# Weight conversion in slices of 768 columns on two engines, and TensorE in program order from the start

## The chip, the cores and the metric

The kernel runs on one core of a Trainium2 chip. The metric is the device time of one execution in microseconds (us). A core has a matrix engine (PE in the profile, with its weight loads as PEld), a vector engine (DVE), a scalar engine (ACT), a general engine (GpSimd, POOL in the profile) and a sync engine (SP) whose queue issues the transfers. Each engine works through its own instructions in order; semaphores make one wait for another.

## The reference

Three stages follow each other: a linear-attention recurrence per batch and head, a gated product, and a second feed-forward stage. All inputs are drawn with `np.random.randn` or `rand`; the weights of the two last stages arrive as float64.

```python
# B=4, H=8, S=768, D=48
for t in range(S):                       # r, k, v, w: [B,H,S,D] float32, u: [H,D]
    y[:, :, t] = r_t @ (state + (u * k_t) v_t)
    state = w_t[:, None] * state + k_t v_t
x = y.transpose(0, 2, 1, 3).reshape(B * S, H * D)      # 3072 x 384
h = ((x @ w1) * (x @ w2)) @ w3                         # w1, w2: 384 x 1024, w3: 1024 x 1024
x = h @ w_out                                          # 1024 x 384
h = x @ w_in                                           # 384 x 2048
g = h * np.clip(h + 3, 0, 6) / 6
return g @ w_out2                                      # 2048 x 384
```

## The kernel before

**Weights.** A float64 weight arrives as two 32-bit words. The kernel converts it on the chip to a float32 bit pattern: `conv`, from the high word `hi` and the low word `lo` of a raw slice. It knows two ways. The *mixed* one uses ACT twice (L98 the magnitude, L99 the sign), DVE three times (L100, L101, L102) and POOL once (L104, a product with the sign). The other one uses ACT once (L106) and DVE four times (L108, L109, L111, L113). The first slice of w3 and of w_out and every second slice of the others go the second way. Weights that are used in several-pass products are then split into a high part by ACT (L116) and a low part by DVE or POOL (L117); a product of split operands is three matmuls (`mm3`, L120 to L122). A `Stream` holds a list of slices and takes each through load, first half (the ACT part) and second half; at most `ahead` slices are between load and end. Slices are 384 or 512 columns.

**Stage A** computes w34 = w3 @ w_out with plain float32 matmuls (L386) while w_out and w3 are converted, and runs the first attention blocks beside it. The w3 slices are `raw_w`/`w3f` in the profile, the w_out ones `raw_wo`/`wo`. Attention is 32 blocks m (a pair of heads, half of a sequence): `load` (wkr, rkv), `prep` (scans e and f, products, the mask A on POOL), `do_kn` (L187), `do_sc` (L198), `do_kv` (L210), `do_y` (L234). Four blocks make one x tile `xt` of 384 tokens.

**Stage B** is the first of eight token blocks bi of the gated product: for each of eight column groups f the products `ab` into two banks, a copy by ACT (L482), the product by DVE (L487), the split into gh and gl (L116, L117), then `out1` with w34 into three accumulators, which ACT copies out at the end (L424). While bi = 0 runs, w1 and w2 (`w12`) are converted. **Stage C** is bi 1 to 5 with attention beside them. **Stage D** is the end of bi 6 and bi 7, with w_in (`wi`) and w_out2 (`wo2`) converted beside them. **Stage E** is the second feed-forward stage, with no conversion left except a little at its start.

**What sets the order.** In stages B to E the PE instructions stand in program order; in stage A a scheduler places them by a simulated time. The other engines are always placed by the scheduler. SP issues the transfers in its order, and a load waits there until its buffer is free.

Of the kernel before, what the change touches and what calls it, by code (L numbers as in the profile page):

```python
# [32 lines left out]
LEAST = float(np.array(0x38000000, np.uint32).view(np.float32))  # L33
MOST = float(np.array(0x47EFFFFF, np.uint32).view(np.float32))
# [8 lines left out]
def pool_split(bi, f):  # L43

    return bi in (0, 1, 7) and f % 2 and f < 7


def build(nc, tc, a):
# [30 lines left out]
    stg = pool("stg", bufs=6, side="left")  # L79
# [12 lines left out]
    def conv(f, raw, late, mixed):  # L92

        lo, hi = raw[..., 0], raw[..., 1]
        fi, ff = f, f.bitcast(F32)
        hf = hi.bitcast(F32)
        if mixed and not late:
            ACT.activation(ff, hf, AF.Abs, scale=2.0 ** -112)  # L98
            ACT.activation(hf, hf, AF.Sign)  # L99
            V.tensor_scalar(out=ff, in0=ff, scalar1=MOST_S, scalar2=None, op0=ALU.min)  # L100
            V.tensor_scalar(out=lo, in0=lo, scalar1=29, scalar2=None, op0=ALU.logical_shift_right)  # L101
            V.scalar_tensor_tensor(out=fi, in0=fi, scalar=3, in1=lo, op0=ALU.logical_shift_left, op1=ALU.bitwise_or)  # L102
        elif mixed:
# [44 lines left out]
    def prep(m):  # L148
# [8 lines left out]
        P_.tensor_copy(stat[:, 1, m], zcols(d1v[i], ZC))  # L157
# [134 lines left out]
    raws, fs = {}, {}  # L292

    def w_load(key, src, n):

        t = stg.tile([128, n, 2], I32, name=f"raw_{key}", tag="raw")
        if len(src.shape) == 3:
            k = src.shape[0]
            nc.sync.dma_start(t.rearrange("p (k m) t -> p k (m t)", k=k), src.rearrange("k p m -> p k m").bitcast(I32))
        else:  # L300
            nc.sync.dma_start(t, src.bitcast(I32).rearrange("p (m t) -> p m t", t=2))
        raws[key] = t

    def w_conv(key, n, late, mixed, hi=None, lo=None, eng=None, dst=None):
        if not late:
            fs[key] = stg.tile([128, n], I32, name=f"f_{key}", tag="f") if dst is None else dst()
            conv(fs[key], raws[key], False, mixed)
        else:
            conv(fs[key], raws.pop(key), True, mixed)
            if dst is None:  # L310
                split(hi, lo, fs.pop(key).bitcast(F32), eng)
# [34 lines left out]

    ear = pool("ear", bufs=2, side="left")
# [4 lines left out]
    def w3_at(q, c0, c1):  # L352
        if q not in w3s:
            w3s[q] = ear.tile([128, 512], I32, name=f"w3f_{q}", tag="w3f", bufs=6)
        return w3s[q][:, c0:c1]

    for q in range(2 * NF1):
        fh, j = divmod(q, NF1)
        if fh == 0:
            args.append((f"wo_{j}", DM, a["w_out"][j], j > 0, None, None, None, lambda j=j: wo[:, j]))  # L360
        for c0, c1 in (((0, 512),) if q else ((0, 128), (128, 512))):
            args.append((f"w3_{q}_{c0}", c1 - c0, a["w3T"][j, :, 512 * fh + c0:512 * fh + c1], q > 0, None, None, None,
                         lambda q=q, c0=c0, c1=c1: w3_at(q, c0, c1)))
    e3 = Stream(args, 4)
# [16 lines left out]


    def w34(fh, j, f4, w3):
        g = fh * 4 + f4
        ps = bank[g % 5][:, :DM]
        mm(ps, w3[:, 128 * f4:128 * f4 + 128], wo[:, j].bitcast(F32), start=j == 0, stop=j == NF1 - 1)  # L386
        if j == NF1 - 1:
            split(w34h[:, g], w34l[:, g], ps)

    e3.upto(3)  # L390
    first = prep(0)
    for q in range(2 * NF1):
        fh, j = divmod(q, NF1)
# [10 lines left out]
    w12p = pool("w12p", bufs=1, side="left")  # L404
    w12h = w12p.tile([128, NF1, 2, KT, 128], F32R, name="w12h")
    w12l = w12p.tile([128, NF1, 2, KT, 128], F32R, name="w12l")
    w12 = Stream([(f"w12_{f}_{s}", DM, a["w2" if s else "w1"][:, :, 128 * f:128 * f + 128], s,
                   w12h[:, f, s].rearrange("p k m -> p (k m)"), w12l[:, f, s].rearrange("p k m -> p (k m)"),
                   P_ if s == 0 else None)
                  for f in range(NF1) for s in range(2)])  # L410
    w12.upto(2)
# [31 lines left out]
    def win_start():  # L443
# [4 lines left out]
        p2["l"] = wp.tile([128, NF2, KT, 128], F32R, name="wil")  # L448
        p2["wi"] = Stream([(f"wi_{j}", DM, a["w_in"][:, :, 128 * j:128 * j + 128], j % 2,
                            p2["h"][:, j].rearrange("p k m -> p (k m)"), p2["l"][:, j].rearrange("p k m -> p (k m)"),  # L450
                            None if j % 2 else P_) for j in range(NF2)])
        p2["wo"] = Stream([(f"wo2_{j}", DM, a["w_out2"][j], j % 2, wo2h[:, j], wo2l[:, j], None if j % 2 else P_)
                           for j in range(NF2)], 1)

# [277 lines left out]
```

## Time and profile before

| what | us |
|---|---|
| median of 3 runs | 962.64 (961.16 to 965.11) |
| profiled execution | 961.57 |
| its span in the trace | 959.8 |
| PE busy | 880.5 (92%) |
| DVE busy | 556.1 (58%) |
| ACT busy | 374.3 (39%) |
| POOL busy | 257.9 (27%) |

The profiled execution lies 1.07 us below the median; its span is 1.8 us shorter than its time. Busy shares are averages over stages that are limited by different engines, so the rows below are taken stage by stage. On DVE, ACT and POOL an instruction's listed duration overlaps the next one's a little; the distance from one start to the next is what an instruction costs when the engine never waits.

### The profile page before, as it was taken

The page shows a single profiled execution, that of the slowest core. Times are in us where ns is not written, and L with a number is a line of the kernel's source. Part 1 is how long each engine was busy: PE and PEld are TensorE (multiplying, and loading weights), DVE is VectorE, ACT ScalarE, POOL GpSimd, SP SyncE. Part 2 cuts the span into 40 slices and gives each one's busy share as a digit, 9 for nine tenths or more (in the row PEclk, how much of TensorE's full clock was granted, in tenths as well). Part 3 has the DMA queues.
Part 4 walks back from the last instruction along what each step waited for, and adds up shares of the span by engine and source line. Part 5 has one row for each costly group of instructions (what it writes and reads, how often), then busy time and mean ns, then how long its engine had stood idle before and what let it go on. Part 6 is the DMA issues. An engine that isn't in the chain of part 4 may idle for free.

```text
span 959.8 us, 13483 instructions
## 1 busy us (share of the span) xinstructions
PE 880.5 (92%) x5074; PEld 744.9 (78%) x5074; DVE 556.1 (58%) x938; ACT 374.3 (39%) x876; POOL 257.9 (27%) x297
## 2 busy tenths in 40 slices
PE   4678677999999999999987899999999999999997
PEld 2344566899889999998877788888888888888885
DVE  8999799565665757575599833433433433333332
ACT  5445553333323333333456533333433433333332
POOL 4988556343332424242155400000000000000000
PEclk9798899999999999999998999999999999999998
DMA  9685466451434334342146410100100000000001
GB/s 277 212 242 167 140 201 186 107 155 56 138 95 125 112 103 134 107 130 79 38 127 211 137 37 1 33 33 0 66 1 1 34 1 0 33 1 1 34 0 37
DMA packets 40762, 86.18 MB, mean 90 GB/s; under 512 B 4352, under 2 KB 20208, under 8 KB 40688
## 3 DMA queue, kind: packets, MB, share of 16 engines
q1 hardware_dynamic: 40688, 85.23, 29.8%
q8 instruction: 42, 0.69, 0.3%
q14 instruction: 32, 0.26, 0.1%
HBM read 66.34 MB, written 9.44 MB: 79 GB/s over the span
## 4 chain that ended last, share of the span: by engine, by line
PE 69%; DVE 17%; DMA 7%; issue 2%; POOL 2%; ACT 2%; SPq 0%; ACTq 0%; POOLq 0%; DVEq 0%
PE bank L120 21%; PE bank L121 21%; PE bank L122 21%; DMA wkr<-in_wkr 4%; PE abank L234 3%; PE abank L198 2%; DVE f L159 1%; DMA raw_w<-in_w 1%; DVE e L155 1%; POOL w3f L104 1%; DMA raw_wo<-in_w_out 1%; DVE w12l L117 1%; DVE raw_w L101 1%; DVE a L487 1%; DVE wil L117 1%
## 5 line engine op out<-in xcount | busy, mean ns | idle before, releaser
L544 DVE SCALAR_TENSOR_TENSOR q<-q,bank 128x512 f32<-128x512 f32 x96 | 66.1, 688 | 193.7 <-ACT q L543 193.6
L120 PE MATMUL bank<-xt,w12h 128*128 128x384 f32 x384 | 137.3, 358 | 11.4 <-ACT w12h L116 5.4
L543 ACT ACTIVATE q<-bank,half 128x512 f32<-128x512 f32 x96 | 66.1, 688 | 189.8 <-PE bank L122 189.8
L122 PE MATMUL bank<-xt,w12l 128*128 128x384 f32 x384 | 131.5, 342 | 0.0
L121 PE MATMUL bank<-xt,w12h 128*128 128x384 f32 x384 | 131.5, 342 | 0.0
L120 PE MATMUL bank<-x,wih 128*128 128x512 f32 x288 | 115.0, 399 | 0.0
L122 PE MATMUL bank<-x,wil 128*128 128x512 f32 x288 | 114.7, 398 | 0.0
L121 PE MATMUL bank<-x,wih 128*128 128x512 f32 x288 | 114.3, 397 | 0.0
L121 PE MATMUL bank<-gl,w12h 128*128 128x512 f32 x288 | 112.7, 391 | 0.0
L122 PE MATMUL bank<-gh,w12l 128*128 128x512 f32 x288 | 112.5, 391 | 0.0
L120 PE MATMUL bank<-gh,w12h 128*128 128x512 f32 x288 | 112.2, 390 | 0.0
L117 DVE TENSOR_TENSOR gl<-q,gh 128x512 fp32r<-128x512 f32 x96 | 66.5, 692 | 65.6 <-ACT gh L116 65.6
L120 PEld LDWEIGHTS bank<-xt,w12h 128*128 128x128 f32 x384 | 74.5, 194 | 18.6 <-DVE a L487 7.6
L116 ACT CAST gh<-q 128x512 fp32r<-128x512 f32 x96 | 59.7, 622 | 65.6 <-DVE q L544 65.6
L121 PE MATMUL bank<-gl,w34h 128*128 128x384 f32 x192 | 66.8, 348 | 17.5 <-DVE gl L117 16.4
L386 PE MATMUL bank<-wo,w3f 128*128 128x384 f32 x128 | 55.7, 592 | 24.6 <-POOL w3f L104 17.7
L121 PEld LDWEIGHTS bank<-xt,w12h 128*128 128x128 f32 x384 | 74.8, 195 | 0.0
L122 PEld LDWEIGHTS bank<-xt,w12l 128*128 128x128 f32 x384 | 74.2, 193 | 0.0
L176 POOL TENSOR_SCALAR_AFFINE_SELECT A<-sd 128x384 f32<-128x384 f32 x64 | 45.3, 731 | 99.7 <-PE abank L234 89.8
L116 ACT CAST gh<-a 128x384 fp32r<-128x384 f32 x64 | 32.7, 510 | 93.6 <-DVE a L487 93.4
L120 PE MATMUL bank<-gh,w34h 128*128 128x384 f32 x192 | 67.3, 351 | 2.0 <-ACT gh L116 2.0
L122 PE MATMUL bank<-gh,w34l 128*128 128x384 f32 x192 | 66.3, 345 | 0.0
(128 smaller groups left out, 1601.1 us busy)
## 6 DMA issues: line engine op xcount, KB each, us to landing
wkr<-in_wkr SPq DMA_DIRECT2D x32, 505.8 KB, 4.6
rkv<-in_rkv SPq DMA_DIRECT2D x32, 432.0 KB, 6.0
raw_wo<-in_w_out SPq DMA_DIRECT2D x24, 384.0 KB, 4.1
raw_w<-in_w3T SPq DMA_DIRECT2D x15, 512.0 KB, 6.7
xt<-y SPq DMA_DIRECT2D x48, 144.0 KB, 4.9
raw_w<-in_w SPq DMA_DIRECT2D x16, 384.0 KB, 3.7
raw_wi<-in_w_in SPq DMA_DIRECT2D x16, 384.0 KB, 4.1
x1d<-x SPq DMA_DIRECT2D x8, 576.0 KB, 5.0
```

The lines of the kernel that those rows point to most:

```text
L101: V.tensor_scalar(out=lo, in0=lo, scalar1=29, scalar2=None, op0=ALU.logical_shift_right)
L116: ACT.copy(hi, src)
L117: (eng or V).tensor_tensor(out=lo, in0=src, in1=hi.bitcast(F32), op=ALU.subtract)
L120: mm(ps, wh, xh, start=first, stop=False)
L121: mm(ps, wh, xl, start=False, stop=False)
L122: mm(ps, wl, xh, start=False, stop=last)
L176: P_.affine_select(out=A[:, j], in_=sd[:, :, j].unsqueeze(2).to_broadcast([128, NC, C]), pattern=[[0, NC], [-1, C]], compare_op=ALU.is_equ ...
L198: mm(ps[j][:, c], d["k"][rows[j], t], d["r"][rows[j], t], start=True, stop=True)
L234: mm(pc[rows[j], c], left, right, start=not started[j], stop=True, skip_group_check=True)
L386: mm(ps, w3[:, 128 * f4:128 * f4 + 128], wo[:, j].bitcast(F32), start=j == 0, stop=j == NF1 - 1)
L543: ACT.activation(q, ps, AF.Relu, bias=half, scale=1.0 / 6.0)
L544: V.scalar_tensor_tensor(out=q, in0=q, scalar=1.0, in1=ps, op0=ALU.min, op1=ALU.mult)
```

## The change

- Every slice has 768 columns. w3 comes in three passes over its tiles of w34 (3, 3 and 2 tiles), so eight slices of 768 columns and four of 512; w_out is four slices, w1/w2 eight, w_in eight, w_out2 eight. The host lays each slice out so that a partition's part is contiguous.
- One way of converting: ACT writes the scaled magnitude (`conv_a`) and, from the top byte of the high word, a number from which the lowest bits come, into `lo`; DVE limits, shifts and joins in three instructions (`conv_b`). POOL takes no part in conversion, splits nothing, and no longer copies the statistics (`stat`, now by ACT).
- Three buffers for raw slices instead of six, three for converted w3 slices instead of six (of 512 columns), and `ahead` is 3 instead of 4 for w3 and w_out.
- PE stands in program order in stage A too.
- The buffers of the split w1/w2 are allocated before those of w_out and w3 instead of after them.

```diff
-def pool_split(bi, f):
-
-    return bi in (0, 1, 7) and f % 2 and f < 7
+NW = 768
+PASSES = ((0, 3), (3, 3), (6, 2))
...
-    stg = pool("stg", bufs=6, side="left")
+    stg = pool("stg", bufs=3, side="left")
...
-    def conv(f, raw, late, mixed):
+    def conv_a(f, raw):
 
         lo, hi = raw[..., 0], raw[..., 1]
...
+        ACT.activation(f.bitcast(F32), hi.bitcast(F32), AF.Abs, scale=2.0 ** -112)
+        top = raw.rearrange("p n t -> p (n t)").bitcast(mybir.dt.uint8).rearrange("p (n b) -> p n b", b=8)[:, :, 3]
+        ACT.activation(lo, top, AF.Copy, scale=1.0 / 32, bias=-15.5 / 32)
+
+    def conv_b(f, raw):
+
+        lo, hi, ff = raw[..., 0], raw[..., 1], f.bitcast(F32)
+        V.tensor_scalar(out=ff, in0=ff, scalar1=MOST_S, scalar2=None, op0=ALU.min)
+        V.scalar_tensor_tensor(out=f, in0=f, scalar=3, in1=lo, op0=ALU.logical_shift_left, op1=ALU.bitwise_or)
+        V.scalar_tensor_tensor(out=f, in0=hi, scalar=-0x80000000, in1=f, op0=ALU.bitwise_and, op1=ALU.bitwise_or)
...
-        P_.tensor_copy(stat[:, 1, m], zcols(d1v[i], ZC))
+        ACT.copy(stat[:, 1, m], zcols(d1v[i], ZC))
...
+    w12p = pool("w12p", bufs=1, side="left")
...
-    e3 = Stream(args, 4)
+    e3 = Stream(args, 3)
...
-    e3.upto(3)
+    order = tc.manual_schedule(engines={mybir.EngineType.PE})
+    order.__enter__()
...
     first = prep(0)
-    for q in range(2 * NF1):
-        fh, j = divmod(q, NF1)
-        e3.upto(2 * q + 7 if fh == 0 else 2 * NF1 + j + 5)
-        w3 = w3s.pop(q).bitcast(F32)
-        for f4 in range(4):
-            w34(fh, j, f4, w3)
-            if f4 == 1 and q < 4:
-                next(first, None)
-            if (4 * q + f4) % 3 == 0 and q >= 4:
+    i = 0
+    for g0, n in PASSES:
+        for jp in range(NF1 // 2):
+            e3.upto(2 * i + 3 if g0 == 0 else NF1 // 2 + i + 2)
+            w3 = w3s.pop(i).bitcast(F32).rearrange("p (j g m) -> p j g m", j=2, m=128)
+            for j in range(2):
+                for g in range(n):
+                    mm(bank[(g0 + g) % 5][:, :DM], w3[:, j, g], wo[:, 2 * jp + j].bitcast(F32), start=jp + j == 0,
+                       stop=jp == NF1 // 2 - 1 and j == 1)
+            i += 1
+            if g0 == 0:
+                next(first, None)
+            else:
                 pull(0)
+                if jp % 2:
+                    pull(0)
+        for g in range(g0, g0 + n):
+            split(w34h[:, g], w34l[:, g], bank[g % 5][:, :DM])
     pull_all(0)
...
-    w12.upto(2)
+    w12.upto(1)
...
-            split(gh, gl, at, P_ if pool_split(bi, f) else None)
+            split(gh, gl, at)
...
-                p2["wi"].upto(2 * (f - FW))
+                p2["wi"].upto(f - FW)
```

What this does to the order on the engines is seen at three places. In all three a name is a tile with its number: w3f_2 is the third slice of w3, wo_107 or wo_112 the whole of w_out, and e_2, f_2 and wkr_2 belong to attention block 2.

The first place is DVE in stage A, at the conversion of the third slice of w3. Before:

```order
L102 SCALAR_TENSOR_TENSOR w3f_2_185<-w3f_2_185,raw_w3_2_0_165 128x512
L155 SCALAR_TENSOR_TENSOR e_2_417<-wkr_2_360,d1c_92 112x388
L117 TENSOR_TENSOR y_0_448<-abank2_68,y_0_448 112x384
L102 SCALAR_TENSOR_TENSOR wo_107<-wo_107,raw_wo_3_174 128x384
L156 RECIPROCAL d1v0_94<-e_2_417 112x3
L169 TENSOR_TENSOR wkr_2_360<-wkr_2_360,e_2_417 112x384
L101 TENSOR_SCALAR raw_w3_3_0_182<-raw_w3_3_0_182 128x512
L159 SCALAR_TENSOR_TENSOR f_2_421<-wkr_2_360,d1v0_94 112x388
L100 TENSOR_SCALAR w3f_3_215<-w3f_3_215 128x512
L217 SCALAR_TENSOR_TENSOR s_1_462<-kvs1_97,pb1_99 112x240
```

and with the change, at the second and third slice of w3:

```order
L99 TENSOR_SCALAR w3f_1_165<-w3f_1_165 128x768
L100 SCALAR_TENSOR_TENSOR w3f_1_165<-w3f_1_165,raw_w3_1_153 128x768
L101 SCALAR_TENSOR_TENSOR w3f_1_165<-raw_w3_1_153,w3f_1_165 128x768
L99 TENSOR_SCALAR wo_112<-wo_112 128x768
L100 SCALAR_TENSOR_TENSOR wo_112<-wo_112,raw_wo_2_160 128x768
L101 SCALAR_TENSOR_TENSOR wo_112<-raw_wo_2_160,wo_112 128x768
L99 TENSOR_SCALAR w3f_2_195<-w3f_2_195 128x768
L100 SCALAR_TENSOR_TENSOR w3f_2_195<-w3f_2_195,raw_w3_2_168 128x768
L101 SCALAR_TENSOR_TENSOR w3f_2_195<-raw_w3_2_168,w3f_2_195 128x768
L99 TENSOR_SCALAR wo_112<-wo_112 128x768
L100 SCALAR_TENSOR_TENSOR wo_112<-wo_112,raw_wo_3_190 128x768
L101 SCALAR_TENSOR_TENSOR wo_112<-raw_wo_3_190,wo_112 128x768
```

Before, the conversion of a slice stands between the scans and products of attention; now ten slices follow each other, three instructions each, and the attention of the next blocks stands ahead of them and behind them.

The second place is SP, which issues the loads, about where w3's later slices come. Before:

```order
L301 DMA raw_w3_8_0_297<-in_w3T 128x1024
L301 DMA raw_w3_9_0_305<-in_w3T 128x1024
L136 DMA wkr_5_611<-in_wkr 112x1156
L138 DMA rkv_5_613<-in_rkv 128x864
L301 DMA raw_w3_10_0_347<-in_w3T 128x1024
L301 DMA raw_w3_11_0_356<-in_w3T 128x1024
L251 DMA xt_0_0_451<-y_2_625 48x768
L251 DMA xt_0_0_451<-y_2_625 16x768
L251 DMA xt_0_0_451<-y_2_625 32x768
L301 DMA raw_w3_12_0_390<-in_w3T 128x1024
L301 DMA raw_w3_13_0_399<-in_w3T 128x1024
L136 DMA wkr_6_696<-in_wkr 112x1156
```

and with the change:

```order
L292 DMA raw_w3_6_241<-in_w3 128x1536
L292 DMA raw_w3_7_249<-in_w3 128x1536
L292 DMA raw_w3_8_274<-in_w3 128x1024
L292 DMA raw_w3_9_317<-in_w3 128x1024
L292 DMA raw_w3_10_381<-in_w3 128x1024
L292 DMA raw_w3_11_432<-in_w3 128x1024
L124 DMA wkr_3_389<-in_wkr 112x1156
L126 DMA rkv_3_391<-in_rkv 128x864
L239 DMA xt_0_0_406<-y_0_403 48x768 x2
L292 DMA raw_w12_0_675<-in_w12 128x1536
L124 DMA wkr_4_469<-in_wkr 112x1156
L126 DMA rkv_4_471<-in_rkv 128x864
```

Before, the attention loads (wkr, rkv) of blocks 5 and 6 stand between loads of w3; now all loads of w3 stand ahead of wkr_3, and the loads of w1/w2 (raw_w12) begin before wkr_4.

The third place is DVE about the last split of attention block 3 (y_3), whose result completes the first x tile and so the first `ab` product. Before:

```order
L200 COPY_PREDICATED A_4_645<-mask_91,abank1_67 128x384
L156 RECIPROCAL d1v1_95<-e_5_672 112x3
L169 TENSOR_TENSOR wkr_5_611<-wkr_5_611,e_5_672 112x384
L101 TENSOR_SCALAR raw_w3_10_0_347<-raw_w3_10_0_347 128x512
L117 TENSOR_TENSOR y_3_710<-abank2_68,y_3_710 112x384
L159 SCALAR_TENSOR_TENSOR f_5_676<-wkr_5_611,d1v1_95 112x388
L100 TENSOR_SCALAR w3f_10_393<-w3f_10_393 128x512
L117 TENSOR_TENSOR w34l_81<-bank0_61,w34h_80 128x384
```

and with the change:

```order
L101 SCALAR_TENSOR_TENSOR f_w12_2_703<-raw_w12_2_690,f_w12_2_703 128x768
L99 TENSOR_SCALAR f_w12_3_766<-f_w12_3_766 128x768
L147 SCALAR_TENSOR_TENSOR f_5_616<-wkr_5_561,d1v1_95 112x388
L105 TENSOR_TENSOR w12l_108<-f_w12_1_687,w12h_107 128x768
L100 SCALAR_TENSOR_TENSOR f_w12_3_766<-f_w12_3_766,raw_w12_3_706 128x768
L105 TENSOR_TENSOR w12l_108<-f_w12_2_703,w12h_107 128x768
L154 TENSOR_TENSOR wkr_5_561<-wkr_5_561,f_5_616 112x384
L101 SCALAR_TENSOR_TENSOR f_w12_3_766<-raw_w12_3_706,f_w12_3_766 128x768
L99 TENSOR_SCALAR f_w12_4_846<-f_w12_4_846 128x768
L105 TENSOR_TENSOR y_3_647<-abank2_68,y_3_647 112x384
L205 SCALAR_TENSOR_TENSOR s_4_658<-kvs0_96,pb0_98 112x240
```

Before, w1 and w2 came later on this engine: the first of their low parts (w12l) stood 59 instructions behind y_3. Now three slices of w1/w2 are done ahead of y_3 and the next two are begun, so that y_3 itself stands at the end of the conversions. On PE, the matmuls of the first pass over w3 now all stand ahead of the first attention block's, of which before the first stood in second place.

## Rows read from the trace of the kernel before

Each group is a view of the profiled execution of the kernel before; durations in the groups of tiles are in ns, times in us.

**Rows 1.** Busy time by engine in stretches of the span, granted PE clock, DMA share.

```profile
core 0: us, PE busy (x) PEld busy (x) DVE busy (x) ACT busy (x) POOL busy (x), PEclk, DMA share, GB/s
0.00:24.00 24.00, 11.50 (x70) 6.86 (x70) 19.30 (x44) 12.31 (x32) 11.76 (x23) 1.00 0.94 277
24.00:96.00 72.00, 54.67 (x252) 31.11 (x252) 71.59 (x111) 33.87 (x89) 63.28 (x53) 0.86 0.69 207
...
110.60:168.00 57.40, 45.38 (x320) 40.73 (x322) 56.26 (x104) 28.22 (x76) 33.69 (x34) 0.90 0.62 180
168.00:186.50 18.50, 16.53 (x115) 15.09 (x116) 12.21 (x21) 4.99 (x16) 7.28 (x10) 1.00 0.40 101
186.50:446.50 260.00, 256.19 (x2041) 238.73 (x2040) 162.40 (x280) 89.42 (x298) 86.80 (x136) 1.00 0.39 110
...
470.70:550.70 80.00, 65.41 (x330) 60.94 (x328) 72.88 (x133) 48.48 (x105) 42.03 (x32) 0.94 0.44 139
550.70:959.80 409.10, 401.92 (x1736) 327.60 (x1736) 139.41 (x204) 142.54 (x225) 0.00 (x0) 0.99 0.06 19
```

**Rows 2.** Waits from 24 to 110 us: total, times, longest.

```profile
PE bank L386 <- POOL w3f L104: 17.7, 9, 4.5
```

**Rows 3.** Timeline, four single instructions: start, duration, engine, idle before.

```profile
110.66 0.66 PE L120 MATMUL bank<-xt,w12h 128*128 128x384 f32 x1 [5.35 <-ACT w12h L116]
...
186.56 0.48 ACT L424 COPY x<-bank 128x384 f32<-128x384 f32 x1 [2.56 <-PE bank L122]
...
470.75 0.56 DVE L117 TENSOR_TENSOR gl<-a,gh 128x384 fp32r<-128x384 f32 x1 [0.58 <-ACT gh L116]
...
550.12 0.54 DVE L117 TENSOR_TENSOR gl<-a,gh 128x384 fp32r<-128x384 f32 x1
```

**Rows 4.** Tile raw_w, ns min/median/max; last line: transfers, us to landing.

```profile
L101 DVE TENSOR_SCALAR raw_w<-raw_w x23: 347/417/2651, 21.2 to 134.6; 128x512 int32<-128x512 int32 x15, 128x384 int32<-128x384 int32 x8
...
L98 ACT ACTIVATE w3f<-raw_w x15: 651/678/733, 18.3 to 87.6; 128x512 f32<-128x512 f32 x15
L102 DVE SCALAR_TENSOR_TENSOR w3f<-w3f,raw_w x15: 657/679/1770, 22.8 to 95.0; 128x512 int32<-128x512 int32 x15
L104 POOL TENSOR_TENSOR w3f<-w3f,raw_w x15: 1272/1352/5863, 26.4 to 99.8; 128x512 f32<-128x512 f32 x15
...
L111 DVE SCALAR_TENSOR_TENSOR f_w<-raw_w,f_w x8: 543/555/1367, 97.1 to 138.2; 128x384 int32<-128x384 int32 x8
...
DMA to landing us min/median/max: 3.1/4.5/11.0
```

**Rows 5.** Lines by form, DVE, 24 to 96 us: busy, mean ns.

```profile
L102 DVE SCALAR_TENSOR_TENSOR w3f<-w3f,raw_w 128x512 int32<-128x512 int32 x14 | 12.1, 866 | 0.0
...
L100 DVE TENSOR_SCALAR wo<-wo 128x384 f32<-128x384 f32 x5 | 3.4, 680 | 0.0
```

**Rows 6.** Lines by form, DVE, 186.5 to 446.5 us (stage C).

```profile
L166 DVE TENSOR_TENSOR wkr<-wkr,f 112x384 f32<-112x384 f32 x20 | 17.6, 882 | 0.2
```

**Rows 7.** Tile wkr, a product on DVE, ns min/median/max.

```profile
L166 DVE TENSOR_TENSOR wkr<-wkr,f x32: 526/981/2069, 12.1 to 453.5; 112x384 f32<-112x384 f32 x32
```

**Rows 8.** Timeline of DVE, 93.6 to 97 us, with no idle time between.

```profile
93.66 0.42 DVE L100 TENSOR_SCALAR w3f<-w3f 128x512 f32<-128x512 f32 x1
93.99 0.55 DVE L166 TENSOR_TENSOR wkr<-wkr,f 112x384 f32<-112x384 f32 x1
...
95.00 0.68 DVE L102 SCALAR_TENSOR_TENSOR w3f<-w3f,raw_w 128x512 int32<-128x512 int32 x1
95.60 0.35 DVE L100 TENSOR_SCALAR f_w<-f_w 128x384 f32<-128x384 f32 x1
...
96.40 0.55 DVE L102 SCALAR_TENSOR_TENSOR f_w<-f_w,raw_w 128x384 int32<-128x384 int32 x1
96.87 0.35 DVE L101 TENSOR_SCALAR raw_w<-raw_w 128x384 int32<-128x384 int32 x1
```

**Rows 9.** DMA issues: KB each, median us to landing.

```profile
xt<-y SPq DMA_DIRECT2D x48, 144.0 KB, 4.9
```

More of the change, by code (lines that the diff above doesn't have):

```diff
@@ L289, in pull_all @@
             pull(limit)
[L292 to L311, printed above, removed]
     class Stream:
@@ L345, in upto @@
                 self.step()
+    w12p = pool("w12p", bufs=1, side="left")
+    w12h = w12p.tile([128, NF1, 2, KT, 128], F32R, name="w12h")
+    w12l = w12p.tile([128, NF1, 2, KT, 128], F32R, name="w12l")
     ear = pool("ear", bufs=2, side="left")
@@ L350, in build, with w3_at @@
     w3s = {}
[L352 to L355, printed above, removed]
-    for q in range(2 * NF1):
-        fh, j = divmod(q, NF1)
[L359 to L363, printed above, removed]
-    e3 = Stream(args, 4)
+    def w3_at(i, n):
+        w3s[i] = ear.tile([128, NW], I32, name=f"w3f_{i}", tag="w3f", bufs=3)[:, :n]
+        return w3s[i]
+    for i, (g0, n) in enumerate((g, n) for g, n in PASSES for _ in range(NF1 // 2)):
+        jp = i % (NF1 // 2)
+        if g0 == 0:
+            args.append((f"wo_{jp}", NW, a["w_out"][jp], lambda jp=jp: wo[:, 2 * jp:2 * jp + 2].rearrange("p j c -> p (j c)")))
+        args.append((f"w3_{i}", 256 * n, a["w3"][i][:, :256 * n],
+                     lambda i=i, n=n: w3_at(i, 256 * n)))
+    e3 = Stream(args, 3)
     e3.load()
@@ L380, in build @@
     V.memset(half, 0.5)
[L383 to L388, printed above, removed]
-    e3.upto(3)
-    first = prep(0)
-    for q in range(2 * NF1):
-        fh, j = divmod(q, NF1)
-        e3.upto(2 * q + 7 if fh == 0 else 2 * NF1 + j + 5)
-        w3 = w3s.pop(q).bitcast(F32)
-        for f4 in range(4):
-            w34(fh, j, f4, w3)
-            if f4 == 1 and q < 4:
+    order = tc.manual_schedule(engines={mybir.EngineType.PE})
+    order.__enter__()
+    w12 = Stream([(f"w12_{f}", NW, a["w12"][f], (w12h[:, f].rearrange("p s k m -> p (s k m)"),
+                                                 w12l[:, f].rearrange("p s k m -> p (s k m)"))) for f in range(NF1)])
+    first = prep(0)
+    i = 0
[8 more added lines that the diff above has]
+            i += 1
+            if g0 == 0:
                 next(first, None)
-            if (4 * q + f4) % 3 == 0 and q >= 4:
+            else:
                 pull(0)
+                if jp % 2:
+                    pull(0)
+        for g in range(g0, g0 + n):
+            split(w34h[:, g], w34l[:, g], bank[g % 5][:, :DM])
     pull_all(0)
     close("ear")
[L404 to L410, printed above, removed]
-    w12.upto(2)
+    w12.upto(1)
     x1p = pool("x1p", bufs=1, side="left")
@@ L448, in win_start @@
         p2["l"] = wp.tile([128, NF2, KT, 128], F32R, name="wil")
[L449 to L453, printed above, removed]
+        p2["wi"] = Stream([(f"wi_{j}", NW, a["w_in"][j],
+                            tuple(p2[x][:, 2 * j:2 * j + 2].rearrange("p j k m -> p (j k m)") for x in "hl"))
+                           for j in range(NF2 // 2)])
+        p2["wo"] = Stream([(f"wo2_{j}", NW, a["w_out2"][j],
+                            tuple(x[:, j].rearrange("p s k m -> p (s k m)") for x in (w12h, w12l)))
+                           for j in range(NF2 // 2)], 1)
     x1s = {}
@@ L646, in general @@
                 for f in range(NF1):
-                    for s, w in enumerate((w1, w2)):
+                    for s in range(2):
                         for kc in range(KT):
-                            mm(bank[s][:, :T1], w[:, f, 128 * kc:128 * kc + 128], x[:, kc], start=kc == 0,
+                            mm(bank[s][:, :T1], w12[:, f, s, kc], x[:, kc], start=kc == 0,
                                stop=kc == KT - 1)
```

109 lines of the change are left out of this document (47 added, 62 removed).

## The prediction

> **What bounds the kernel now.** I read the busy times by stretch first [rows 1]. From 186.5 to 446.5 us PE is busy 256.19 of 260 us at the full clock, and from 550.7 to the end 401.92 of 409.1 us: stages C and E belong to PE and hold no conversion, so the change finds nothing there to save. It can act in three stretches only. From 24 to 96 us DVE is busy 71.59 of 72 us, POOL 63.28, PE only 54.67; from 110.6 to 168 us DVE is busy 56.26 of 57.4 and PE 45.38; from 470.7 to 550.7 us DVE is busy 72.88 of 80 and PE 65.41. In all three DVE is the engine that never rests. The waits agree only in part: PE's longest wait in stage A is for POOL, the sign product L104, 17.7 us in 9 pieces [rows 2]. POOL is thus the second suspect, and the two are coupled. The same DVE shift takes 347 ns at least and 2651 at most, the POOL product 1272 and 5863 [rows 4]: when both are at work, both get slow.
>
> How much that stretching is worth comes from the rows by form. In 24 to 96 us the ten costliest DVE forms reach from L102 on w3f, 14 times at a mean of 866 ns, to L100 on wo, 5 times at 680 [rows 5]; for L102 the least is 657 [rows 4], so it loses 14 x 0.209 = 2.9 us. The same difference over all forms of that view gives about 23 of the 72 us. In stage C, where POOL does only attention's work, the largest stretch is that of L166, a mean of 882 ns [rows 6] over a least of 526 [rows 7]; over all forms it is 14.6 us for 20 attention blocks, 0.73 us for one.
>
> The marks of the stages: the first `ab` matmul starts at 110.66 after PE waited for ACT's w12h; the x1 copy of block 0 starts at 186.56; gl of block 6, f 3 at 470.75, gl of block 7, f 7 at 550.12 [rows 3].
>
> **The price of an instruction.** From start to start on a DVE that never waits [rows 8], 512 columns cost 0.33 us for a tensor_scalar (93.66 to 93.99) and 0.60 for L102 (95.00 to 95.60), 384 columns 0.47 for L102 (96.40 to 96.87). So 128 columns more are 0.13, and 768 columns cost 0.60 + 2 x 0.13 = 0.86; the tensor_scalar I take as 0.48. The bounds for 768 are 0.60 (as 512) and 1.2 (twice 512 of its kind); the line through two sizes decides. A new slice is then 0.48 + 0.86 + 0.86 = 2.2 us on DVE, 3.06 with the split's 0.86. ACT reads 512 strided columns in 678 ns [rows 4]; 768 lie between that and 1.02, I take 0.9, so 1.8 us for the two instructions of a slice. The byte read with a stride of 8 bytes has no row; I take it as the word read. Twice as slow would be 2.7 us a slice, still under DVE's 3.06 with a split.
>
> **Removed and added in DVE's own instructions.** By these prices a pair of old slices (one mixed, one not) costs 2.95 us with splits where POOL takes half the work, and the new slice of the same columns 3.06. DVE's instructions do not get fewer in time: w_out and w3 go from 29.9 to 32.7 us. What is removed is POOL's sign product with its stretching of DVE, and PE's wait for it. Nothing else pays.
>
> **Stage A.** In the new order of DVE I add up all rows from the first conversion to the low part of y_3: 12 slices of 768 without splits 26.4, four of 512 (0.33 + 0.60 + 0.60) 6.2, w1/w2 slices 0 to 2 with splits 9.2 and the parts of 3 and 4 2.7, attention 28.3 (six blocks of scans and products at 3.2, the rest masks, s and y), six w34 splits 2.8: 75 us. To that comes: the start, 6.3 (786 KB at 277 GB/s with a DMA share of 0.94 [rows 1], so about 300 at full share, 2.6 us, some 2 to get going, 0.9 for ACT and queueing behind the second load); waits for loads, 12; and stretching by POOL's remaining work. The loads: three buffers turn over in 0.4 of issue, 4.4 of landing, 1.8 of ACT, 1.7 of DVE, 8.3 / 3 = 2.8 us a slice against DVE's 2.2, ten slices in a row: 5.5; w3_1 stands on SP behind five attention loads, 1.5; wkr_3 stands behind all loads of w3 and reaches DVE late, 2; w12_2 and wkr_5, 3. Bounds for the sum are 0 and 20. Stretching: 0.73 us for a block is the least; all of POOL's own work for a block is the most, 3.0 us where nothing stretches it (in stage C 86.80 / 20 = 4.3 busy, four gl splits among it [rows 1]); I take 1.5 x 4.3 blocks = 6.5. So y_3 ends near 6.3 + 75 + 12 + 6.5 = 99.8. Its transfer to xt lands after 4.9 [rows 9]: first `ab` near 104.5, 6 us earlier. The weights are no longer what it waits for.
>
> **Stage B.** From there to gl of block 0, f 7, DVE's rows add up to 52 us (four blocks of attention, 16 products and gl splits, w1/w2 4 to 7, 2.5 slices of w_in). With 6 of stretching, 4 of waits and the 5.4 that pass from the last gl to the copy now (two gaps of PE work), the copy of x1 is at 99.8 + 52 + 15.4 = 167. PE's own way: 45.38 + 16.53 = 62 us busy from 110.6 to 186.5, some of it at a clock of 0.90, so 58 at the full one, 162 to 166. DVE still sets the end, barely. From 186.56 to 167: **-19.5 us** for A and B together.
>
> **Stages C and E: 0.** Here the gl splits of block 1 go from POOL to DVE, which is busy 162.4 of 260; the cover is PE's work. The copy of the statistics moves to ACT, busy 89.4 of 260.
>
> **Stage D.** From gl_6_3 to gl_7_7 the rows of the new order add up to 55.4 us (5 slices of w_in and 8 of w_out2 at 3.06, 24 products and splits, the x1 splits); by the same prices those of before add up to 53.0, in the 79.4 us that it took [rows 3]. POOL has nothing left to do, so no stretching; waits for loads (one buffer ahead for w_out2) 5, for PE in its order 3: 63.5 to 64. PE's own floor is 65.41 x 0.94 = 61.5. So **-15.5 us**. This part is limited twice, so it has little more to give.
>
> **The sum.** 961.57 - 19.5 - 15.5 = 926.6; the median lies 1.07 above the profiled execution: **927**.
>
> [...] The row L101 says 347 to 2651 ns while POOL works [rows 4]. [...]
> The row L111, which reads one operand at every second word, takes 543 ns at 384 columns at least [rows 4], hardly more than the contiguous L166 with 526 [rows 7]. [...]
>
> **Rivals.**
> - *DVE's stretching goes entirely, loads keep up.* POOL's work falls between DVE's waits. Then y_3 is at 6.3 + 75 + 5 = 86, `ab` at 92, x1 at 151 (PE's floor), stage D at 60: -36 - 19 = -55, **906**. For it: POOL falls from 63 to about 15 us of work in stage A. Against: the load ring is slower than DVE by my count.
> - *What POOL still does shuts DVE out in full.* 3.0 us a block instead of 1.5: +6.5 in A, +6 in B; first `ab` at 111, x1 at 180; with little else in D: **941**. For it: L101 at 2651. Against: stage C.
> - *The stretching was never POOL's.* Then 23 / 72 of stage A stays, +16 in A, +3 in B, D gains half: **955**.
> - *Slower: the ring of three buffers.* If a load lands not in 4.4 but in 11.0 us, the longest that raw_w shows [rows 4], a slice turns over in (0.4 + 11 + 1.8 + 1.7) / 3 = 5.0 us instead of 2.8. Ten slices in stage A that nothing covers lose 2.2 each, eight beside attention (3.9 of DVE work each) 1.1, sixteen in D (4.0 each) 1.0: 47 us given back against 35 won, **974**. It decides from a landing of about 10 us, 4.7 us a slice. For it: six buffers become three, and slices double. Against: the median landing is 4.5 with four in flight [rows 4], and the stretch 24 to 96 moves 207 GB/s at a DMA share of 0.69 [rows 1], so a third is free.
>
> **How the numbers follow.** Chances: the forecast (915 to 938) 0.50; stretching gone (about 906) 0.17; shut out in full (about 941) 0.18; never POOL's (955) 0.06; the ring (974) 0.07; the strided operands cost more after all, 0.02. The range is 902 to 956: it leaves out the ring, the strided operands, half of the 955 case and a quarter of the lowest, 0.16 in all. What a measurement of this kernel can tell from no change is about 0.5%, 4.8 us; so faster 0.90, within it 0.03 (part of the 955 case and the strided one), slower 0.07.
>
> **What the changed profile would show.** Right: L100 and L101 of the change near 0.9 us each at 768 columns with few over 1.5; PE no longer waiting for POOL in stage A but for DVE; first `ab` at 100 to 108 with y_3's transfer as its releaser; the x1 copy of block 0 at 160 to 172; C within 2 us of 260; gl_6_3 to gl_7_7 in 61 to 67. Wrong: DVE idle for loads in stage A over 20 us (the ring); means over 1.2 us for L100 (POOL, or the strided operand); stage D still over 70, which would mean that PE's order and DVE wait on each other there.

## The result, and the profile after

The changed kernel takes 935.12 us (median of 4 runs, 934.42 to 939.49) against 963.59 for the one before (4 runs): a ratio of 0.971, 95% interval 0.967 to 0.975. The change is faster by 28 us; 927 was forecast for a kernel of 962.64, a gain of 36. The profiled execution (939.49, span 937.7) lay 4.4 us above the median. A second profile of the same kernel, the run `again` below, took 932.23 with a span of 930.5; where one number is given for the changed kernel it is from that second one, and the first is set beside it where it differs.

Stretches of the changed kernel's second profile, with columns as in [rows 1]: the start, stage A, stage B from the point at which the first `ab` product goes on with the last third of its x rows (the "second group" of the expectations below) to the x1 copy, stage C, stage D from gl of block 6, f 3 to gl of block 7, f 7, stage E from the x1 copy of block 7 on.

```profile
0.00:24.00 24.00, 6.33 (x12) 3.26 (x12) 19.12 (x31) 10.83 (x29) 10.96 (x19) 1.00 0.95 327
24.00:96.00 72.00, 57.14 (x322) 35.04 (x323) 62.10 (x93) 39.14 (x80) 22.20 (x26) 0.88 0.64 203
108.00:173.60 65.60, 58.77 (x428) 53.70 (x429) 53.99 (x86) 30.48 (x80) 17.33 (x21) 0.93 0.52 162
173.60:433.40 259.80, 256.35 (x2040) 238.70 (x2039) 163.35 (x283) 91.35 (x319) 75.82 (x113) 1.00 0.39 110
457.70:522.70 65.00, 59.78 (x330) 56.34 (x328) 55.32 (x83) 43.75 (x69) 0.00 (x0) 1.00 0.44 146
523.90:930.50 406.60, 400.00 (x1734) 325.22 (x1733) 142.20 (x208) 144.73 (x228) 0.00 (x0) 0.99 0.07 23
```

POOL falls from 63.28 to 22.20 us of the 72 between 24 and 96 (the forecast spoke of about 15), and DVE, which had no rest there, now has 10 us of it. Stage C is the same to 0.2 us. Single instructions of the same execution, from the timelines of PE, DVE and ACT:

```profile
97.26 0.63 PE L108 MATMUL bank<-xt,w12h 128*128 128x384 f32 x1
...
102.28 0.54 DVE L105 TENSOR_TENSOR y<-abank,y 112x384 fp32r<-112x384 f32 x1
...
107.95 0.66 PE L108 MATMUL bank<-xt,w12h 128*128 128x384 f32 x1 [9.18 <-DMA xt<-y]
...
173.60 0.48 ACT L399 COPY x<-bank 128x384 f32<-128x384 f32 x1 [2.56 <-PE bank L110]
```

The product starts at 97.26 with the rows of x that the first three attention blocks have filled, and then stands 9.18 us for those of the fourth: y_3's low part starts on DVE at 102.28, and its transfer lets the product go on at 107.95. Before, the product started at 110.66 and waited for weights [rows 3]; y_3 had been there long since (DVE's timeline of the kernel before):

```profile
74.55 0.54 DVE L117 TENSOR_TENSOR y<-abank,y 112x384 fp32r<-112x384 f32 x1
```

The change thus moves y_3 back by 28 us, and most of what stage A won is lost in front of one tile.

| where | before | forecast | after |
|---|---|---|---|
| y_3's low part on DVE, start (forecast: end) | 74.6 | 99.8 | 102.3 |
| the `ab` product runs from | 110.7 | 104.5 | 108.0 |
| x1 copy of block 0 | 186.6 | 167 | 173.6 |
| stage C, to the copy of block 5 | 259.95 | 260 | 259.8 |
| gl_6_3 to gl_7_7 (stage D) | 79.4 | 63.5 to 64 | 65.0 |
| last x1 copy to the end (stage E) | 408.4 | 408.4 | 406.6 |

The changes add up: -13.0 to the first x1 copy, -14.4 in stage D, -1.8 in stage E, 0 elsewhere, 29.3 us between the spans 959.8 and 930.5. In the first profile of the changed kernel the same terms are -11.3, -11.8 and -1.7, and stage C with the front of block 6 is 2.8 longer; PE's granted clock there is 0.97 in stage D and 0.90 in stage B, where the second shows 1.00 and 0.93.

### The profile page after: what moved, and what is told of

Read it like the earlier page. It is cut to its first block, busy times and chain, and to the rows that moved or that the text cites. A ratio compares the mean times of both kernels' runs of the same rounds, so it can differ in the third digit from the quotient of the medians.

```text
span 937.7 us, 13091 instructions
## 1 busy us (share of the span) xinstructions
PE 873.4 (93%) x5074; PEld 741.8 (79%) x5074; DVE 521.2 (56%) x821; ACT 376.5 (40%) x845; POOL 134.4 (14%) x186
## 3 DMA queue, kind: packets, MB, share of 16 engines
q1 hardware_dynamic: 27744, 85.23, 29.3%
## 5 line engine op out<-in xcount | busy, mean ns | idle before, releaser
L105 DVE TENSOR_TENSOR gl<-q,gh 128x512 fp32r<-128x512 f32 x96 | 66.4, 692 | 64.2 <-ACT gh L104 64.2
L108 PEld LDWEIGHTS bank<-xt,w12h 128*128 128x128 f32 x384 | 73.7, 192 | 17.7 <-DMA xt<-y 8.5
L373 PE MATMUL bank<-wo,w3f 128*128 128x384 f32 x128 | 53.3, 575 | 26.0 <-DVE w3f L101 25.3
L109 PEld LDWEIGHTS bank<-xt,w12h 128*128 128x128 f32 x384 | 73.7, 192 | 0.1
L373 PEld LDWEIGHTS bank<-wo,w3f 128*128 128x128 f32 x128 | 28.0, 227 | 47.1 <-DVE w3f L101 26.5
```

The source lines that it names most:

```text
L105: (eng or V).tensor_tensor(out=lo, in0=src, in1=hi.bitcast(F32), op=ALU.subtract)
L108: mm(ps, wh, xh, start=first, stop=False)
L109: mm(ps, wh, xl, start=False, stop=False)
L373: mm(bank[(g0 + g) % 5][:, :DM], w3[:, j, g], wo[:, 2 * jp + j].bitcast(F32), start=jp + j == 0, stop=jp == NF1 // 2 - 1 and j == 1)
```

## The experiments

Twelve runs, each with four or more timed executions and at least as many of the kernel before on the same chip. Ratios are to the kernel before.

**again** (no edit).

> The changed kernel once more, for a second profile, since the profiled execution lay 4 us above the median of its runs. Every theory: a median of 933 to 937. If the 4 us were a disturbance of that execution, the marks of stage A or B move by about as much (the second group of the first ab product near 106 to 110, the x1 copy of block 0 near 171 to 175) and the others stay; if they are spread over the span, all marks shift a little.

933.61 us, 0.970 (0.966 to 0.974). The median is as expected. The 7.2 us between the two spans are spread: 1.6 at the x1 copy of block 0, 1.1 more by the end of stage C, 4.3 in the rest up to the last x1 copy, 0.1 after it.

**pool_beside**: work for POOL beside every conversion.

```diff
                 conv_b(f, self.raw.pop(i))
+                ff = f.bitcast(F32)
+                P_.tensor_tensor(out=junk[:, :n], in0=ff, in1=ff, op=ALU.mult)
```

> The changed kernel with a product on POOL added for every converted slice, whose result nobody reads: POOL's traffic comes back, no wait for POOL. If the gain came from POOL leaving DVE alone: before, DVE lost 23 us in 24 to 96 us beside 63 us of POOL work, 0.37 us for one; forty products of about 2 us are 80 us, and what of them lies in stages A, B and D (most) gives back 15 to 25 us: 950 to 960, with the means of the DVE conversions over 1.1 us in stage A. If the gain came from larger slices, buffers or PE's order: within 3 us of the changed kernel, 932 to 938.

961.33 us, 0.999 (0.997 to 1.001): the whole gain is gone, a little more than the first theory gave. The extra products on the slices of w3 and of w1/w2, by tile (those on w_out, w_in and w_out2 are twenty more):

```profile
L311 POOL TENSOR_TENSOR junk<-w3f x12: 1036/1649/2233, 14.2 to 97.5; 128x768 f32<-128x768 f32 x8, 128x512 f32<-128x512 f32 x4
L311 POOL TENSOR_TENSOR junk<-f_w x8: 1468/1916/3122, 98.6 to 144.5; 128x768 f32<-128x768 f32 x8
```

and the first join of a w3 slice on DVE between 24 and 96 us by form, first in this run, then in the changed kernel:

```profile
L101 DVE SCALAR_TENSOR_TENSOR w3f<-w3f,raw_w 128x768 int32<-128x768 int32 x7 | 9.9, 1419 | 0.3
```

```profile
L100 DVE SCALAR_TENSOR_TENSOR w3f<-w3f,raw_w 128x768 int32<-128x768 int32 x7 | 6.7, 957 | 0.8 <-ACT raw_w L94 0.6
```

No engine waits for the product; the only waits for POOL listed are DVE's for attention's own product, 8.0 us in all against 6.4 in the changed kernel. The same DVE instruction takes 1419 instead of 957 ns on average. The loss lies where conversions are: the profiled spans differ by 25.3 us, 17.6 of it up to the first x1 copy and 10.0 in stage D. A part of it goes with PE's granted clock: in stage B it is 0.86 here against 0.93, and PE is busy 63.06 us against 58.82. 27.7 us for 40 products of 1.85 us on average are 0.7 us each, 0.37 us of the kernel's time for one of POOL; the expectation had taken 0.37 of DVE's time for one, from the kernel before. The work put back is not the work that was removed, since POOL is busy 35.89 us between 24 and 96 here and was busy 63.28 before; that the two times agree to 0.1% is chance.

**sign_on_pool**: the old mixed conversion in every second slice.

```diff
-    def conv_b(f, raw):
+    def conv_b(f, raw, mixed=False):
...
+        if mixed:
+            V.tensor_scalar(out=ff, in0=ff, scalar1=MOST_S, scalar2=None, op0=ALU.min)
+            V.tensor_scalar(out=lo, in0=lo, scalar1=29, scalar2=None, op0=ALU.logical_shift_right)
+            V.scalar_tensor_tensor(out=f, in0=f, scalar=3, in1=lo, op0=ALU.logical_shift_left, op1=ALU.bitwise_or)
+            P_.tensor_tensor(out=ff, in0=ff, in1=hi.bitcast(F32), op=ALU.mult)
+            return
```

> The changed kernel with the old mixed conversion (sign product on POOL) in every second slice: DVE does 0.4 us less work in 20 slices, 8 us, POOL gets 20 products that PE and the splits wait for. If POOL's sharing is the price: half of what the added products cost comes back, and waits for POOL, against 8 saved: 935 to 948. If sharing costs nothing: the 8 us show, 925 to 930.

943.76 us, 0.980 (0.976 to 0.985), by the first theory. Less work for DVE and yet 10 us slower than the changed kernel: taking back half of the old trade loses. How much of the 10 us is stretching and how much the waits for POOL that come back with it was not separated.

**old_slices**: the kernel before with only the new conversion and no POOL in conversion, splits and statistics.

```diff
-            P_.tensor_tensor(out=ff, in0=ff, in1=hf, op=ALU.mult)
...
+            V.tensor_scalar(out=ff, in0=ff, scalar1=MOST_S, scalar2=None, op0=ALU.min)
+            V.scalar_tensor_tensor(out=f, in0=f, scalar=3, in1=lo, op0=ALU.logical_shift_left, op1=ALU.bitwise_or)
+            V.scalar_tensor_tensor(out=f, in0=hi, scalar=-0x80000000, in1=f, op0=ALU.bitwise_and, op1=ALU.bitwise_or)
```

> The kernel before with one part of the change alone: the new conversion and splits without POOL, in the old slices of 384 and 512 columns, with six buffers, PE scheduled in stage A and w1/w2 converted after w3. A pair of half slices costs DVE 3.34 us by the spacings instead of 3.06. If POOL leaving is the gain: most of it comes, 935 to 945. If it is slices, buffers and order: 955 to 965.

932.02 us, 0.968 (0.963 to 0.974). This part alone gives what the whole change gives, and more than was expected of it. Larger slices, fewer buffers, PE in program order and the earlier room for w1/w2 are worth nothing that can be measured when all are taken together; the runs below show that single ones cost and that the rest can pay. Its x1 copy of block 0 is at 172.62, as in the changed kernel, though its `ab` product starts at 100.32, 7.6 us earlier.

**raw4**: four raw buffers, four slices under way.

```diff
-                self.raw[i] = stg.tile([128, NW, 2], I32, name=f"raw_{key}", tag="raw")[:, :n]
+                self.raw[i] = stg.tile([128, NW, 2], I32, name=f"raw_{key}", tag="raw", bufs=4)[:, :n]
...
-    e3 = Stream(args, 3)
+    e3 = Stream(args, 4)
```

> The changed kernel with four buffers for raw slices instead of three, and four slices under way for w3 and w_out. DVE stood 15.5 us in stage A of the changed profile, about 8 of them behind raw slices that had not landed or were not yet read by ACT. If the ring of three is what cost stage A its gain: the second group of the first ab product 5 to 8 us earlier, 926 to 930. If the loads are late because of their place in SP's order and the attention's place in DVE's: 932 to 936.

932.99 us, 0.968 (0.964 to 0.971), as the changed kernel. DVE's longest wait for a w3 slice shrinks from 4.4 to 2.8 us, but y_3 goes later (106.03), since more of w1/w2 is converted ahead of it, and `ab` goes on at 113.01 instead of 107.95. The x1 copy stays at 173.37.

**pe_sched**: PE placed by the scheduler in stage A.

```diff
-    order = tc.manual_schedule(engines={mybir.EngineType.PE})
-    order.__enter__()
...
+    order = tc.manual_schedule(engines={mybir.EngineType.PE})
+    order.__enter__()
     prev = None
     quota = 0.0
```

> The changed kernel with PE placed by the scheduler in stage A, as before: attention's matmuls come back between those of the first pass over w3, and wkr_3, wkr_4 stand ahead of w3's middle slices on SP. If program order on PE put attention late in stage A and so made y_3 late: y_3 3 to 8 us earlier, 926 to 931. If DVE's own work sets y_3: 932 to 936, with the x1 copy of block 0 within 2 us.

924.23 us, 0.960 (0.957 to 0.963): 9.4 faster than the changed kernel, by the first theory. The timelines of DVE, PE and ACT in this run:

```profile
94.23 0.55 DVE L105 TENSOR_TENSOR y<-abank,y 112x384 fp32r<-112x384 f32 x1
...
98.48 0.69 PE L108 MATMUL bank<-xt,w12h 128*128 128x384 f32 x1 [6.47 <-DMA xt<-y]
...
165.28 0.48 ACT L395 COPY x<-bank 128x384 f32<-128x384 f32 x1 [2.56 <-PE bank L110]
```

y_3 is 8.0 us earlier, `ab` 9.5, the x1 copy 8.3. DVE has not done less for it; the first 140 us of this run, and of the changed kernel:

```profile
0.00:140.00 140.00, 107.94 (x609) 76.90 (x610) 124.94 (x193) 78.59 (x176) 58.79 (x59) 0.90 0.70 235
```

```profile
0.00:140.00 140.00, 93.09 (x527) 64.26 (x528) 124.06 (x184) 77.44 (x171) 47.22 (x57) 0.89 0.71 228
```

DVE is busy 124.94 against 124.06 us, PE 107.94 against 93.09: nearly the same time on DVE, but PE has done 15 us more.

**early**: attention pulled in the first pass over w3, PE still in program order.

```diff
-    first = prep(0)
+    for _ in prep(0):
+        pass
...
-            if g0 == 0:
-                next(first, None)
-            else:
-                pull(0)
-                if jp % 2:
-                    pull(0)
+            pull(0)
+            if jp % 2:
+                pull(0)
```

> The changed kernel with attention pulled already in the first pass over w3, PE in program order: y_3 stands 26 rows earlier on DVE, the last w3 slices later. If the order of stage A is what is lost: y_3 ends 8 to 15 us earlier, and the x1 copy of block 0 3 to 8 us earlier, 925 to 930. If DVE's total work up to the last gl of block 0 sets the copy: y_3 earlier, the copy not, 932 to 936; w34's later end could even cost 2 to 5.

929.94 us, 0.967 (0.964 to 0.970), at the upper edge of the first theory. y_3 starts at 80.38, 22 us earlier, more than the 8 to 15 expected. `ab` no longer waits for it but 3.12 us for the last w34 split (at 101.66); the x1 copy is at 168.94.

**w12_late**: the buffers of w1/w2 after those of w_out and w3.

```diff
-    w12p = pool("w12p", bufs=1, side="left")
...
     close("ear")
+    w12p = pool("w12p", bufs=1, side="left")
```

> The changed kernel with the buffers of w1/w2 allocated after those of w_out and w3 again: fewer w1/w2 conversions stand ahead of y_3 (6 rows of DVE fewer), the others follow later. By DVE's total work the x1 copy of block 0 stays within 2 us, the first ab product about 4 us earlier and then waits for weights: 932 to 937. If it is the wait for the first x tile that costs (PE stands 8 us for y_3 in the changed profile): 926 to 930.

926.51 us, 0.963 (0.960 to 0.966): 7 us faster, by the second theory. y_3 starts at 96.18 instead of 102.28; `ab` runs from 99.82, after a wait of 3.92 us for the first weights, and the x1 copy is at 165.83. The first theory, that DVE's total work keeps the copy where it was, fails here.

**pe_and_w12, pe_w12_ring, pe_w12_wo2**: both parts undone together; the same with four raw and five w3 buffers; the same with two w_out2 slices under way.

```diff
-    stg = pool("stg", bufs=3, side="left")
+    stg = pool("stg", bufs=4, side="left")
...
-                           for j in range(NF2 // 2)], 1)
+                           for j in range(NF2 // 2)], 2)
```

> The changed kernel with two of its parts undone together: PE placed by the scheduler in stage A, and the buffers of w1/w2 after those of w_out and w3. Each alone gave about 9 and 7 us, and in both the first ab product came 8 to 10 us earlier and the x1 copy of block 0 followed it by 66 to 67 us. If both act through the same thing, the time at which y_3 completes the first x tile: about as good as the better one, 921 to 926, with ab near 96 to 99. If they act apart: 916 to 920.

> As the run with both parts undone, and with the room that this frees: four raw buffers, four slices under way, five converted w3 slices. Four raw buffers alone changed nothing. If loads limit stage A once attention stands better: 3 to 6 us faster than without; if DVE's work does: within 2 us.

> As the run with both parts undone, with two w_out2 slices under way in stage D instead of one. DVE stood 6 us in stage D behind ACT's first step on w_out2 slices that had landed late. If that is on the path: 2 to 4 us faster; if PE's own work sets stage D (busy 61 of 68 us): within 2 us.

928.55 us, 0.962 (0.960 to 0.965); 928.95, 0.963 (0.960 to 0.966); 929.80, 0.965 (0.960 to 0.970). The first misses both its numbers: together the two are worse by 4 us than PE's order undone alone. PE's timeline in it:

```profile
95.54 0.44 PE L108 MATMUL bank<-xt,w12h 128*128 128x384 f32 x1 [4.07 <-ACT w12h L104]
...
100.01 0.69 PE L110 MATMUL bank<-xt,w12l 128*128 128x384 f32 x1 [3.83 <-DVE w12l L105]
```

x is there at 95.5, but the weights are not: `ab` stops once for the high part and, at its third matmul, for the low part. More buffers and a second w_out2 slice change nothing beyond that, by the second expectation of each.

**pe_sched_early**: PE scheduled, attention pulled early, w1/w2 early (the edits of pe_sched and early).

> The changed kernel with PE placed by the scheduler in stage A and attention pulled already in the first pass over w3, w1/w2 still allocated early. On DVE y_3 now stands 21 rows ahead of the first low part of w1/w2 instead of 7 behind it. If the first ab product starts with the later of the two, y_3's transfer and the first w1/w2 slice, it now waits for the slice, about where y_3's transfer ended in the run with PE scheduled alone: ab at 95 to 99, 922 to 928. If only y_3 counted: ab near 88 to 92 and 915 to 919.

923.94 us, 0.959 (0.955 to 0.962), the best kernel of this study, level with pe_sched. The time is that of the first theory, its reason is not: `ab` waits neither for y_3 (77.34) nor for the first w1/w2 slice (low part done at 93.07). PE's timeline:

```profile
87.63 7.08 PE L370 MATMUL bank<-wo,w3f 128*128 128x384 f32 x16 [3.33 <-DVE w3f L101]
94.26 0.63 PE L108 MATMUL bank<-xt,w12h 128*128 128x384 f32 x1
```

PE comes straight from the last matmuls of w34, and what it had waited for there is a w3 slice on DVE.

## Why the prediction came out as it did

**What the gain is made of: right, and shown for the stretching.** "What is removed is POOL's sign product with its stretching of DVE, and PE's wait for it. Nothing else pays." POOL work put back without any wait for it takes all of the gain away (961.33), and the removal alone, in the old slices, gives all of it (932.02). The rival that the stretching was never POOL's is out. What PE's wait of 17.7 us was worth by itself is open: it goes in old_slices together with the stretching. "Nothing else pays" is right of the sum only, and there with luck: two parts cost 9.4 and 7.1 us, and with PE's order undone the larger slices, the fewer buffers and the early room stand 8 us below old_slices (924.23 against 932.02, intervals 0.957 to 0.963 and 0.963 to 0.974).

**How much POOL's remaining work stretches DVE: right.** 1.5 us for a block was taken, between 0.73 and 3.0. In the changed kernel between 24 and 96 us, the DVE forms that lose most:

```profile
L143 DVE TENSOR_TENSOR_SCAN e<-wkr,d1c 112x388 f32<-112x388 f32 x3 | 4.0, 1334 | 0.0
...
L147 DVE TENSOR_TENSOR_SCAN f<-wkr,d1v 112x388 f32<-112x388 f32 x3 | 3.8, 1258 | 0.0
...
L101 DVE SCALAR_TENSOR_TENSOR f_w<-raw_w,f_w 128x768 int32<-128x768 int32 x3 | 3.7, 1243 | 0.0
L157 DVE TENSOR_TENSOR wkr<-wkr,e 112x384 f32<-112x384 f32 x4 | 3.4, 854 | 0.0
```

Above the least durations of these forms (941, 952 and 521 ns in the kernel before, 926 for L101 in this one) they lose 3 x 0.39, 3 x 0.31, 3 x 0.32 and 4 x 0.33 us, 4.4 for three to four blocks; the same difference over all forms of the stretch is some 6 us. Neither of the two rivals on this (gone, or 3.0 us a block) fits.

**The price of a slice on DVE: low by 0.3 us.** 0.48 + 0.86 + 0.86 = 2.2 came from rows in which each instruction stood among others. In the changed order the three of a slice follow each other on the same tile (DVE's timeline, first profile):

```profile
27.78 0.55 DVE L99 TENSOR_SCALAR w3f<-w3f 128x768 f32<-128x768 f32 x1
28.42 0.96 DVE L100 SCALAR_TENSOR_TENSOR w3f<-w3f,raw_w 128x768 int32<-128x768 int32 x1
29.41 0.96 DVE L101 SCALAR_TENSOR_TENSOR w3f<-raw_w,w3f 128x768 int32<-128x768 int32 x1
30.29 0.55 DVE L99 TENSOR_SCALAR wo<-wo 128x768 f32<-128x768 f32 x1
```

From start to start 0.64, 0.99 and 0.88, 2.51 together: here the instruction that reads the one before it starts after that has ended (listed end 29.38, start 29.41), the independent one before the one ahead of it has (listed end 30.37, start 30.29). Nine slices ahead of y_3 stand like this in the second profile, some 2.7 us. ACT's byte read costs what was taken (0.91 us in the middle for 768 columns). The strided operands on DVE cost here what contiguous ones do: 0.96 us is listed for them above, 0.94 in the middle for the split L105 of 768 columns (tile w12l, same profile).

**Loads: sized right, and the ring is no limit.** DVE's waits in stage A of the changed kernel from 6 to 108 us:

```profile
DVE w3f L99 <- ACT w3f L92: 7.3, 6, 4.4
DVE wo L99 <- ACT wo L92: 2.7, 2, 2.4
DVE e L143 <- DMA wkr<-in_wkr: 0.8, 1, 0.8
```

With three smaller ones it is 12.6, of which 2.4 belong to the start: 10.2 where 12 were taken. A fourth buffer changes nothing in the time (932.99), so the rival of the ring is out. Up to y_3 DVE has this:

```profile
6.00:102.28 96.28, 66.25 (x344) 40.09 (x344) 85.15 (x123) 52.24 (x114) 32.24 (x32) 0.91 0.73 236
```

It is busy 85.15 us where 81.5 (75 and 6.5) were taken, and idle 11.1 where 12 were; the 2.7 us of dependent instructions are most of the difference. The start took 6.0 us, 6.3 were put down, though the parts named for it add up to 5.5. y_3's low part ends at 102.8 instead of 99.8.

**Stage B: the step that was sized wrong.** The -19.5 for A and B measured -13.0: y_3 is 3.0 us late, as above, and DVE's waits from there to the last gl of block 0 are 8.3 us where 4 were taken. DVE's work in this stretch, 57.1 us, fits the 58 (52 and 6), and so do the 5.4 us from the gl to the copy. Of the waits 5.7 are for gh on ACT, 4.5 of them in one piece (timelines of ACT and DVE):

```profile
149.81 0.92 ACT L94 ACTIVATE raw_wi<-raw_wi 128x768 int32<-128x768 uint8 x1 [3.94 <-DMA raw_wi<-in_w_in]
150.62 0.50 ACT L104 CAST gh<-a 128x384 fp32r<-128x384 f32 x1
...
151.15 0.56 DVE L105 TENSOR_TENSOR gl<-a,gh 128x384 fp32r<-128x384 f32 x1 [4.52 <-ACT gh L104]
```

ACT stands 3.94 us for a slice of w_in, reads it, and only then makes the gh that DVE needs: the forecast counted loads for DVE here, not what a late load does to ACT's order.

"DVE still sets the end, barely" is therefore not what the trace shows. From 107.95 to the copy DVE is busy 54.04 of 65.65 us and PE 58.82, and each waits for the other. The chain that ended last, followed back from release to release, lies in this stretch for 24.6 us on PE, 18.6 on transfers (8.6 of them slices of w_in) and 14.6 on DVE; before, it lay for 46.4 of 75.9 us on DVE and 13.5 on PE. Nor does the start of `ab` set the copy alone. The copy follows that start by 65.6 us in the changed kernel, 66.8 with PE scheduled, 66.0 with w1/w2 late and 67.3 with attention early, so in these an earlier start moved it by nearly as much; but it follows by 60.4 us with four buffers and by 72.3 in the old slices, and both have the copy where the changed kernel has it. Which of the waits in stage B decides is open.

The forecast accepted y_3 "at the end of the conversions". Program order on PE and the early room for w1/w2, which put it there, cost 9.4 and 7.1 us by the run in which each is undone alone. In both runs y_3 comes earlier, by 8.0 and 6.1 us, and `ab` with it; undone together they replace the wait for the x tile by one for the weights. That this one tile is the whole of the 9.4 and 7.1 us is argued, not shown, and how the 9.4 divide between PE's own order and the order that it makes DVE and SP take was not separated.

**Stage D: right.** 63.5 to 64 forecast, 65.0 and 67.5 measured in the two profiles (the second first), with PE's waits for DVE's gl down from 9.9 us to 3.8:

```profile
PE bank L109 <- DVE gl L105: 3.8, 6, 1.3
PE bank L108 <- ACT gh L104: 1.8, 3, 0.7
```

PE is busy 59.78 of the 65.0, a little under the floor of 61.5 that was named. Of the 14.4 us 5.6 are PE's own busy time, 65.41 us at a granted clock of 0.94 before [rows 1] against 59.78 at 1.00; the rest is waits.

**Stages C and E:** 0 forecast, -0.2 and -1.8 measured. In stage E PE hardly rests in either kernel, but its first 5 us differ (before, then after):

```profile
551.38:556.38 5.00, 5.00 (x18) 4.17 (x17) 0.00 (x0) 1.75 (x4) 0.00 (x0) 0.66 0.58 208
```

```profile
523.92:528.92 5.00, 5.00 (x24) 4.03 (x22) 1.88 (x3) 3.72 (x6) 0.00 (x0) 1.00 0.81 310
```

Before, the granted clock was 0.66 there and PE did 18 matmuls; after the change it was 1.00 and 24 matmuls. PE had been busy 0.42 of the 2 us from 548 to 550 before, and 1.40 of the 2 us from 527.6 to 529.6, as far ahead of stage E, in the first profile of the changed kernel, where the clock of these 5 us is 1.00 too; that the one sets the other was not shown. At the pace of the rest of the stage, 435 matmuls in 100 us, the six are 1.4 us, most of the 1.8.

The size of the whole was off by 8 us in 36, and that is stages A and B (its own sum gives 927.6, not 927). Of the signs that the forecast named, the x1 copy of block 0 lies outside its 160 to 172, at 173.6 and, in the first profile, 175.2; that profile also misses the 100 to 108 for `ab` (110.3) and the 61 to 67 for stage D (67.5). The others came as named.

## What to carry to other kernels

When an engine is taken off shared work, price the work by what it does to the other engine's instructions, not by its waits: here PE's wait for POOL was 17.7 us, but POOL products that nobody waits for were enough to cost the whole gain (961.33 us). When conversions move, ask which single tile the next stage starts with, and count what stands ahead of its last piece on every engine; here the work of the busiest engine did not tell when that piece is done (DVE busy 124.94 us of the first 140 with PE scheduled and 124.06 without, y_3 at 94.23 and 102.28). Undo the parts of a change one at a time, and then together: one part gave the whole gain, and two others cost 7 and 9 us each, but undoing both gave back only 5.

## What the runs showed of the hardware that was not expected

In the first profile a DVE instruction that reads the result of the one just ahead of it started 0.99 us after it (28.42 to 29.41), where an independent one started 0.88 after (29.41 to 30.29; 768 columns, 0.96 us listed for both). In pool_beside POOL products that nobody waits for cost the kernel 0.37 us for each of their own microseconds (27.7 us for 40 products of 1.85 on average). On ACT, reading single bytes 8 bytes apart cost what reading single words 8 bytes apart did: 907 against 894 ns in the middle, with four slices of 512 columns in each list; for 768 columns alone 911 against 898. The rows are those of tile raw_w in the first profile:

```profile
L94 ACT ACTIVATE raw_w<-raw_w x20: 667/907/941, 8.3 to 117.6; 128x768 int32<-128x768 uint8 x16, 128x512 int32<-128x512 uint8 x4
L92 ACT ACTIVATE w3f<-raw_w x12: 656/894/972, 7.5 to 80.7; 128x768 f32<-128x768 f32 x8, 128x512 f32<-128x512 f32 x4
```
